# A linear attention block and an MLP on one core: another order of the same 1566 turns

## The chip, the core and the metric

The kernel runs on one core of a Trainium2 chip. The core has TensorE for matmuls (PE in the profile; its weight loads are PEld), VectorE (DVE), ScalarE (ACT), GpSimd (POOL), and SyncE (SP), whose queue here issues nearly all DMAs. Each engine works through its own list of instructions in order and waits on semaphores for the others. The metric is the device time of one execution in microseconds.

## The reference, cut to what matters

Gated linear attention keeps a 48x48 state per head, scaled by a gate and added to at every token; then a layer norm and a two-layer MLP with a residual. Four batches of 768 tokens, 8 heads of 48 (384 columns), 1536 hidden columns; the two weight matrices arrive as 64-bit floats.

```python
def _attn_ref(q, k, v, alpha):
    for t in range(S):
        state = alpha[:, :, t, :, None] * state + np.einsum('bhd,bhe->bhde', k[:, :, t], v[:, :, t])
        y[:, :, t] = np.einsum('bhd,bhde->bhe', q[:, :, t], state)

def _moe_ref(x, g_ln, w_ch1, w_ch2):
    mu = np.mean(x, axis=-1, keepdims=True)
    var = np.mean((x - mu) ** 2, axis=-1, keepdims=True)
    xn = (x - mu) / np.sqrt(var + 1e-06) * g_ln
    ch = np.maximum(xn @ w_ch1, 0.0) @ w_ch2
    return (x + ch).astype(np.float32)
```

## The kernel before

The tokens are cut into 6 chunks of 128 for each of 4 batches: 24 attention pieces, named a to x in time order (letter 4c + b for chunk c, batch b). A piece (`attention`, L278) takes the logarithm of its gates (ScalarE, L292), sums them along the tokens by a matmul with a triangle (L298 for chunk 0, L303 later), exponentiates (L306, L307), scales k and q (VectorE, L309, L311), transposes both (L336), forms scores (L352 or L360, one head a time), masks them (L367 or L372), updates the state (ups, L388; L397 or L401 and the gate's product on GpSimd, L403), forms the outputs (yps, L414, or L426 and L429), normalises (L437 to L470), transposes again (L476) and writes the columns of its chunk's xT (L479, L483). The gate of a chunk goes to DRAM as a row and comes back as columns (L316, L378).

The matmuls of single heads, L303, L352, L360, L388, L414, L426 and L429, use 64-row or 64-column tiles of the array, several of them side by side. All others use the whole array.

The MLP needs w1 and w2 in 32 bits. Twelve pieces (A to L: six of w1, then six of w2) are loaded by SP (L205) into three staging buffers and rounded by three VectorE operations, one on ScalarE (L223), and two more on VectorE (L217 to L227). Chunk 0 goes through the MLP in the plain way: hidden columns (L506, turns Y and Z) and projection (L518, turns P and Q). Chunks 1 to 5 use fast block products, with fewer products and more sums: 30 first products a chunk (L795, two matmuls each; turn M, and V for the last chunk) and 20 second products (L618, four matmuls each; turn M). The sums of inputs are VectorE operations on SBUF alone: `combine_first` (L744, S), `combine_x` (L769, X), `combine_weights` (L578, W), `combine_hidden` (L605, N). The sums behind a product read it from PSUM on VectorE or ScalarE (L628 to L678, L803 to L838), and some go on to GpSimd (L634, L814 to L834). R are the ReLUs (L846), O fetches the residual of an output (L493); finished outputs are sent at L497.

What sets the order is one string, ORDER (L25). Each of the functions named above is a generator, and a letter of the string runs its generator to its next `yield`:

```python
    with tc.manual_schedule():
        for turn in ORDER:
            next(turns[turn], None)
```

So the string fixes, for each engine, the order of its instructions, and for SP the order of its DMAs. Buffers rotate in the order in which turns ask for them. All PSUM tiles share eight buffers (`tag="bank", bufs=8`); la, x and xn share eight rows; qT, kT and the sums share eleven; alpha, k and q share six.

Of the kernel before, what the change touches and what calls it, by code (L numbers as in the profile page):

```python
# [22 lines left out]


ORDER = (  # L25
    "acacababcdaacabdbaabdcacabbacbbababceccbaAcfcdbadaacecacfeafdedebdfbeadbaedeecge"
    "adbAacgAfedghbgeedfecfafgfcefdAgeddbbgfdfghffbebaigcjbibffhjBhcdcYhCfcgccehYfedh"
    "cfedeedhgdedYjAfidBfjiBZhjhZZfBYegfhgjhghCiZYBYiCYYhfhghhkggZilihjZjgiZCiDjYDZZZ"
    "ghZYEYjkeiYkiDiEijgljjjlghYCYhiYkhYFEZhiFigYEZigkikDYZZlkkeejlYlgjhFlZlmYkZgknlg"
    "jZSGkHmiknlSljlkiljkjlGiHlmlllZimFhmZYgYmmjZiYhmheeHmGlkfSnZlnZefSQnmfiGHZghkkeo"  # L30
    "IYmSkiISkJgjIjommmOmJPJnSnQgopPghlKPIKhKjiPOnLSnSfSXkmQLffQOLXWkimXPQSWmPPXpnOpW"
    "XmnnXSmXSQomWnnpnmSoXmQMlmlkXkWliMnnMoXXpjWSWSMjMMoMoMlSMnMMWMoMknMMpMMqMMMMMOPi"
    "npnMopMMrmOMjkpMpopopRqoMoirQkplppnqprRppqWMMWMMnMWMqlMRrMMMMkMqRMMMjkrqRMrMMpsk"
    "oMoMMqMMRRnqpMMRjMqMMoWqOqsnRpqlsoqqpMsNtRNpMMNMjNoMoMMMosRqMMMOkNooMqtNMNMMMtMo"
    "MRlNNsmkNMpqMMNtMMMNlMrMMNMMNqMtqMsrMMWNnrrqMMMNMMstnMXvMsMMvXXprXorrXXXrqMMMXXM"
    "MMMMMMMsXqMMOmvMMMMMMMuXMMMMMMmtRMmttMRrtMrMMttrstvMtqussvsqtMMMMqMrMMrvMMMrRMMM"
    "MRMtMnMRMMmssmrMrrpOtsORMuRMoRMsMMMMoRNMMNtMMNMpqMMMoRNMRNMNNMMNRNOMnNMMMrstMpMN"
    "toNMNMMMMMrMnuoOMsMuNMvxMMuMNrpMOMNovMMvMMvMpMMMXtXMxvvMsXvssXXsXtvMXMuMXuXMMMMM"
    "usMMMtwMMMMMMvMMvwuuuRuuXuuuLxvXOMMMMMMMMMMMwMwxMrMuMswMuMMMwMMsvRxRvMMsMMRwMMxM"
    "xMqwMxMMxMwRtMMMxwMMMMxRqruwtxRwxswxxwRxwuxwRMNvNwMRMNrvwNRMMMMMMtNwNNquNNRrsvst"  # L40
    "tMNMJxMOMMMNNMxMMMvMqMuwxxMNtMtMMMMxuwXMwMMNXMXMMNMvNMXXuMXMXMMxXMXwMMXwMMMvMwMM"
    "MxMMMMMMMXMMMMMOuMuMMRMMMMMMMMwMMMMMMMMMRMMvxMMRMRxwMMMROMuMRMvOwxMMRRMwMRxMNMOM"
    "uMvMMXRVNMMMXXMMRMXXXXMMNVNVXVVXMVNMMVVVMVRVNXVVVVVNRVVMNXVVMVRVMVMVNVNMNVVVMVMV"
    "VMRVRVMVVVMVMVONVMVMNMVMMMRVMNNVRVVVVMVVROVMMMVMNVRVVRVMVMVMNMVRKMOMMMRNNMNMMNMM"
    "MMMNVNMNMNVMMMMNRONMMMNMMNMMMNMMMMNMMMNMMMMMMM"
)


# [860 lines left out]
```

## Time and profile before

| | |
|---|---|
| three runs | 434.07, 435.91, 436.53 us, median 435.91 |
| profiled execution, first to last instruction | 431.0 us; the page gives no other time for it, so its own time is known only by this span, 4.9 us under the median |
| TensorE busy | 425.7 us (99%) |
| weight loads busy | 378.2 us (88%) |
| VectorE busy | 333.2 us (77%) |
| ScalarE busy | 200.0 us (46%) |
| GpSimd busy | 152.7 us (35%) |
| granted TensorE clock | 0.999 |
| DMA | 45.53 MB; busy share 0.87 in the first 44 us, 0.64 from 44 to 120 us, 0.24 from 160 to 300 us |

The stages follow each other in TensorE's lines: the first hidden columns of chunk 0 (L506) start at 32.6 us, the projection of chunk 0 (L518) at 85.0, the first fast products (L795) at 123.6, the first second products (L618) at 161.9. Attention pieces lie among them until about 309 us.

A line of the profile names the engine, the line of the kernel and the tile; "x12" counts records, of which a matmul in 32 bits leaves two. The chain of work that ended last is followed back from the last instruction, at each step to what released it. A wait is idle time of an engine, put down to what ended it.

### The profile page before, as it was taken

The numbers are of one execution on the slowest core, as the hardware profiler recorded it, in microseconds if no ns is written. First come the engines' busy times: TensorE is split into PE (matmuls) and PEld (weight loads), VectorE is DVE, ScalarE is ACT, GpSimd is POOL, SyncE is SP. The second block draws the span as 40 slices with busy tenths as digits, with TensorE's granted clock in tenths as the row PEclk, the third lists the DMA queues.
The fourth block names the chain that finished last, engine by engine and source line by source line (L and its number), as shares of the span: only waits on it lengthen the run. The fifth ranks groups of instructions, "written<-read, shape, count | busy, mean of one in ns | idle before, by whom it ended". The sixth has DMA issues, their size and how long they took to land.

```text
span 431.0 us, 11676 instructions
## 1 busy us (share of the span) xinstructions
PE 425.7 (99%) x4760; PEld 378.2 (88%) x4760; DVE 333.2 (77%) x644; ACT 200.0 (46%) x519; POOL 152.7 (35%) x164
## 2 busy tenths in 40 slices
PE   8999999999999999999999999999999999999997
PEld 6788888866588889998889998889998899999996
DVE  4989899999998888866769756757686668948683
ACT  6597466774043882325385134384415562221100
POOL 1011031110205382252563243580153661647423
PEclk9999999999999999999999999999999999999999
DMA  8979968774117354031150141400014000011201
GB/s 287 288 208 272 308 151 257 203 247 142 38 56 212 107 148 141 29 105 45 52 151 23 49 120 38 94 2 22 2 56 146 2 1 2 0 39 37 75 18 55
DMA packets 55517, 45.53 MB, mean 106 GB/s; under 512 B 26748, under 2 KB 51580, under 8 KB 55464
## 3 DMA queue, kind: packets, MB, share of 16 engines
q1 hardware_dynamic: 54920, 44.63, 35.0%
q8 instruction: 37, 0.61, 0.6%
q10 hardware_dynamic: 544, 0.17, 0.2%
q14 instruction: 16, 0.13, 0.1%
HBM read 35.25 MB, written 9.53 MB: 104 GB/s over the span
## 4 chain that ended last, share of the span: by engine, by line
PE 94%; DVE 2%; DMA 1%; ACT 1%; SPq 0%; issue 0%; DVEq 0%
PE hps L795 30%; PE ops L618 30%; PE ops L518 7%; PE hps L506 6%; PE tps L336 4%; PE aps L360 3%; PE ups L388 2%; PE yps L426 2%; PE yps L429 2%; PE xps L476 2%; DMA ws<-in_moe_w_ch_dram 1%; PE lps L303 1%; PE aps L352 1%; PE lps L244 1%; PE lps L298 1%; PE yps L414 1%
## 5 line engine op out<-in xcount | busy, mean ns | idle before, releaser
L795 PE MATMUL hps<-sum,w 128*128 128x256 f32 x192 | 48.0, 381 | 0.0
L634 POOL TENSOR_TENSOR ob<-ob,u 128x192 f32<-128x192 f32 x40 | 27.0, 685 | 58.9 <-DVE ob L631 44.3
L618 PE MATMUL ops<-w,hT 128*128 128x192 f32 x224 | 40.7, 328 | 0.0
L795 PEld LDWEIGHTS hps<-sum,w 128*128 128x128 f32 x192 | 35.7, 190 | 4.7 <-ACT hT L825 0.2
L618 PEld LDWEIGHTS ops<-w,hT 128*128 128x128 f32 x224 | 36.9, 190 | 1.0 <-issue 0.6
L403 POOL TENSOR_TENSOR mid<-mid,gate 112x192 f32<-112x192 f32 x20 | 13.3, 668 | 68.7 <-DVE mid L401 19.7
L795 PE MATMUL hps<-xT,w 128*128 128x256 f32 x136 | 34.4, 380 | 0.0
L506 PE MATMUL hps<-xT,w 128*128 128x256 f32 x144 | 34.0, 384 | 0.1
L846 ACT ACTIVATE hT<-hT 128x512 f32<-128x512 f32 x48 | 28.8, 625 | 10.4 <-POOL hT L817 7.1
L518 PE MATMUL ops<-w,hT 128*128 128x384 f32 x96 | 32.8, 490 | 0.0
L628 DVE TENSOR_TENSOR ob<-ops,ob 128x192 f32<-128x192 f32 x50 | 17.6, 353 | 17.7 <-PE ops L618 9.4
L506 PEld LDWEIGHTS hps<-xT,w 128*128 128x128 f32 x144 | 26.3, 190 | 4.0 <-DVE xT L479 0.6
L618 PE MATMUL ops<-ws,sum 128*128 128x192 f32 x160 | 29.2, 327 | 0.0
L814 POOL TENSOR_TENSOR hT<-hT,u 128x512 f32<-128x512 f32 x8 | 10.4, 1305 | 53.0 <-DVE u L813 53.0
L795 PEld LDWEIGHTS hps<-xT,w 128*128 128x128 f32 x136 | 25.5, 190 | 3.2
L518 PEld LDWEIGHTS ops<-w,hT 128*128 128x128 f32 x96 | 17.6, 190 | 10.5
L618 PEld LDWEIGHTS ops<-ws,sum 128*128 128x128 f32 x160 | 26.4, 190 | 0.2
L336 PE MATMUL tps<-consts,qk 128*112 128x128 f32 x176 | 25.3, 275 | 0.2 <-DVE qk L311 0.2
L336 PEld LDWEIGHTS tps<-consts,qk 128*112 128x112 f32 x176 | 20.3, 134 | 4.3 <-DVE qk L311 0.8
L460 ACT ACTIVATE xn<-x,few 128x384 f32<-128x384 f32 x24 | 14.8, 615 | 18.7 <-DVE few L456 17.5
L618 PE MATMUL ops<-ws,hT 128*128 128x192 f32 x128 | 23.4, 327 | 0.0
L618 PE MATMUL ops<-more,sum 128*128 128x192 f32 x120 | 22.0, 327 | 0.0
(243 smaller groups left out, 1172.9 us busy)
## 6 DMA issues: line engine op xcount, KB each, us to landing
ws<-in_moe_w_ch_dram SPq DMA_DIRECT2D x12, 768.0 KB
vn<-in_v_dram SPq DMA_DIRECT2D x12, 384.0 KB
kept<-x SPq DMA_DIRECT2D x24, 192.0 KB
ob<-kept SPq DMA_DIRECT2D x24, 192.0 KB
out_dram<-ob SPq DMA_DIRECT2D x19, 192.0 KB
ra<-in_alpha_dram SPq DMA_DIRECT2D x14, 192.0 KB
rk<-in_k_dram SPq DMA_DIRECT2D x6, 384.0 KB
rq<-in_q_dram SPq DMA_DIRECT2D x6, 384.0 KB
```

The lines of the kernel that those rows point to most:

```text
L336: nc.tensor.transpose(tps[:, p], qk_of(c, b)[:, i, p].rearrange("p a b -> p (a b)")[:, :R], ident)
L360: nc.tensor.matmul(aps[0][halves[i if cross else 1 - i], p, s], kT[rs, p, s], qT[rs, p, s], start=True, stop=True)
L403: nc.gpsimd.tensor_mul(new, new, by)
L460: act(out=xn, in_=x, func=AFT.Square, bias=mean, accum_out=dev)
L506: nc.tensor.matmul(hps, w1[:, j // 2, f, j % 2 * P:][:, :P], xT_of[0][:, f, bs], start=(f == 0), stop=(f == NF - 1))
L518: nc.tensor.matmul(ops_of[b], hT_of[c][:, j, b], w2[:, j], start=(j == 0), stop=(j == NJ - 1))
L618: nc.tensor.matmul(acc, lhs[:, j], rhs[:, j], start=(j == 0), stop=(j == NT - 1))
L628: nc.vector.tensor_add(x, acc, x)
L634: getattr(nc.gpsimd, f"tensor_{op}")(x, x, y)
L795: nc.tensor.matmul(acc[:, i], w, b, start=True, stop=True)
L814: add_late(c4, c4, u2)
L846: nc.scalar.activation(out=x, in_=x, func=AFT.Relu)
```

## The change

Only the string is another one. Both strings hold the same letters equally often. The letter changes at 1258 of the 1565 places between two turns in the old string and at 854 in the new one, where a letter often stands many times in a row. The new order was chosen with VectorE and GpSimd allowed to work side by side. Cut to a few rows, the first, two of the middle and the last:

```diff
-    "acacababcdaacabdbaabdcacabbacbbababceccbaAcfcdbadaacecacfeafdedebdfbeadbaedeecge"
-    "adbAacgAfedghbgeedfecfafgfcefdAgeddbbgfdfghffbebaigcjbibffhjBhcdcYhCfcgccehYfedh"
...
-    "MRlNNsmkNMpqMMNtMMMNlMrMMNMMNqMtqMsrMMWNnrrqMMMNMMstnMXvMsMMvXXprXorrXXXrqMMMXXM"
-    "MMMMMMMsXqMMOmvMMMMMMMuXMMMMMMmtRMmttMRrtMrMMttrstvMtqussvsqtMMMMqMrMMrvMMMrRMMM"
...
-    "MMMNVNMNMNVMMMMNRONMMMNMMNMMMNMMMMNMMMNMMMMMMM"
+    "acaabaaaabbdbbbcdccaaacabbbadbeaccfbbbabcccceafecdadefAfaabdaabacaaeeaddfdedbeae"
+    "eacccgdddbeAehfgggcebgcbbbhddgdecfAefffgbggbAefefefgdfggffffggBdCjhjccAhcdcYdhdg"
...
+    "MMMMWMNNjjMMrrlqnNNsMMMMMrpnMtNoqMrtqqmrrrnrorrjrtrtrMMMMlooOMNtssjsjmNMXXXXXXXX"
+    "XpMrmMMMMMMMMMsMMvMMMMMrqppMppuMMMXOMMMMMMMtttsstsLsssssvttttXtRtrrttsuuvvRuutsM"
...
+    "OMMMMMMMMMMMMMMMMMOMMMMMMMMMMMMMNNNMMMMMMMMMMM"
```

Since each engine's list follows the string, every engine's list changes its order: TensorE's 2512 matmuls, VectorE's 634 instructions, ScalarE's 471, GpSimd's 164 and SP's 259 DMAs. The products of one chunk keep their order among themselves (`FIRST`, L775, and `SECOND`, L609), as do the operations of one attention piece and of one piece of weights.

## The prediction

> **What bounds the kernel now.** I read the page first: busy times, the 40 slices, the chain that ended last.
>
> ```profile
> PE 425.7 (99%) x4760; PEld 378.2 (88%) x4760; DVE 333.2 (77%) x644; ACT 200.0 (46%) x519; POOL 152.7 (35%) x164
> ...
> PE   8999999999999999999999999999999999999997
> ...
> DVE  4989899999998888866769756757686668948683
> ...
> POOL 1011031110205382252563243580153661647423
> ...
> PE 94%; DVE 2%; DMA 1%; ACT 1%; SPq 0%; issue 0%; DVEq 0%
> ```
>
> TensorE is busy 425.7 of 431.0 us and holds 94% of the chain. A busy PE need not be working at full rate, so I then read what it waited for (the waits with TensorE as the one that waits; this is the whole answer):
>
> ```profile
> PE lps L244 <- DVE more L241: 1.1, 1, 1.1
> PE aps L352 <- DVE kT L341: 0.8, 1, 0.8
> PE tps L336 <- DVE qk L311: 0.2, 1, 0.2
> ```
>
> 2.1 us in all, all before 12 us. Third, the pieces of the chain in order of time. From 43.85 us to 427.9 us every piece is a PE piece. What they show is a price that no wait table has:
>
> ```profile
> 52.60 5.18 PE hps L506 x24
> 59.80 2.79 PE hps L506 x12
> 62.59 1.10 PE yps L426 x58
> ...
> 80.46 2.59 PE hps L506 x12
> ...
> 169.09 0.66 PE lps L303 x3
> ...
> 256.68 0.93 PE yps L426 x58
> ...
> 307.04 1.08 PE yps L429 x64
> 308.12 1.04 PE yps L426 x61
> 309.16 1.50 PE ops L618 x8
> 310.98 11.70 PE ops L618 x72
> ```
>
> Twelve hps records take 2.59 us when what stands before them uses the whole array (the transposes of L336 and L476), but 2.79 behind a run of the small matmuls of one head (59.80). Eight ops records take 11.70 / 72 x 8 = 1.30 in the stream and 1.50 behind small ones (309.16). So coming back from small tiles costs 0.20 us. Going in costs between nothing (1.08 for 64 records first in a run, 1.04 for 61 second) and 0.17 (1.10 for 58 first in a run, 0.93 for 58 inside one). The end is fixed: last VectorE add at 428.0 + 0.36, then 2.6 us until the last output lands.
>
> **The change, part by part.** No instruction is added or removed: 2512 matmuls, 507 VectorE two-tensor operations, 156 GpSimd ones, 259 DMAs from SP in both.
>
> *Fewer changes of tile size.* In the instruction order, the small matmuls (L303, L352, L360, L388, L414, L426, L429) stand in 29 unbroken runs before and 16 after; mean length by the chain's rates goes from some 2.1 to 3.7 us. 13 returns at 0.20 and 13 entries at 0 to 0.17: 2.6 to 4.8 us. I take 0.28 a pair, the middle, since both entry rows occur: 13 x 0.28 = 3.6 us, all of it on the path, since PE is the path. One more run ends with L303 (4 against 3), whose last pair then lies bare (169.09: 0.66 us) where inside a run it overlaps its neighbours: 0 to 0.6 us back, taken as 0.3.
>
> *Longer runs need more banks at once.* All PSUM tiles share eight buffers (tag "bank"). A run with two chunks' lps, aps, two ups and two yps fills them, and the first big product behind it waits for an eviction. Evictions by rows: copy_predicated (L372) 0.73 us, the yps sum (L443) 0.55, the state adds (L401) 0.35. Walking the new order with these durations, there are some eight places, from about 70 us on, where the eviction that frees the bank (or the yps before a projection) stands right ahead of the matmul that needs it. The price of each is between nothing and one whole late eviction, 0.73: 0 to 5.8 us. I take 0.2, nearer the low end, because the order before also has such pairs and no wait on PE came of them: 8 x 0.2 = 1.6 us. What hides it where it costs nothing is VectorE's spare time, 101 of 140 us busy between 160 and 300 us; between 44 and 120 us (70.8 of 76.0) there is hardly any.
>
> *VectorE and GpSimd side by side.* The trace of before shows that they are not free of each other. Two-tensor VectorE operations on SBUF alone, and GpSimd's:
>
> ```profile
> L605 DVE TENSOR_TENSOR sum<-sum,sum x15: 681/684/1539, 174.2 to 423.4; 128x512 f32<-128x512 f32 x15
> ...
> L605 DVE TENSOR_TENSOR sum<-sum,hT x4: 682/884/1757, 185.0 to 389.1; 128x512 f32<-128x512 f32 x4
> ...
> L634 POOL TENSOR_TENSOR ob<-ob,u x40: 587/591/1242, 179.9 to 426.9; 128x192 f32<-128x192 f32 x40
> ```
>
> The columns are minimum, median and maximum in ns. 1757 is 684 plus most of a 1270 ns GpSimd add (L814's median is 1276); VectorE operations that read PSUM keep their time beside GpSimd. A collision so costs the late engine up to 1.3 us, and the order before already has them without a wait on PE. Laying the operations of both orders side by side at their places among the matmuls, 57 two-input operations fall beside a GpSimd one before and 48 after, so I see no more collisions, only less distance where one falls. Bounds: -0.5 (a few fewer) to 8.7 us (worked out below); taken 0, since the count gives no more of them. The Trainium skill, page "SBUF — State Buffer", section "Who interferes with whom", says that a VectorE instruction with two SBUF inputs and a GpSimd instruction that reads SBUF hold one shared read interface in turn, the second fully blocked: it speaks against a plan that lets them run side by side. The 684 and 1757 ns agree with it. By that rule alone each collision costs its whole overlap; by the waits above it costs PE nothing until it meets a short distance.
>
> *The head.* First transposes wait for the same q load (VectorE's 8.03 us operation): 8.7 us against 8.64. The kT copies now stand ahead of the third k product, so the first L352 can start 0.6 us earlier than 11.47. The weight loads keep their places in SP's queue: pieces 0 to 5 are SP's 22nd, 47th, 53rd, 55th, 67th and 68th DMA (before: 20, 47, 55, 62, 65, 73). Piece 3 goes ahead of the alpha, k and q of a chunk, so those are up to 2.6 us late (768 KB at the 308 GB/s of the page's busiest slice); between load and first use the new order leaves them 6 us or more of PE work at that place. Piece 1's rounding has six VectorE operations between its halves instead of three, some 1.4 us more, against a PE use that is 3 us of matmuls behind. Ends: -0.6 to +2.6 us, taken 0, being hidden on the rows just named. SP's queue loses no DMA, and what waits behind a blocked one there is what waited before. The tail has the same last products and the same sends: 0.
>
> *Sum.* -3.6 + 0.3 + 1.6 = -1.7 us on the profiled span: 431.0 to 429.3. The median of the three runs is 435.9, 4.9 above the span; I leave that alone: 435.9 - 1.7 = 434.2 us.
>
> **The rivals.**
>
> *All of the saving arrives.* If no bank is late, only 13 pairs count: -3.6, with the entries dear -4.8, minus 0.3 for L303: 432.3, down to 431.4. For it: VectorE has a quarter of its time free after 160 us. Against: between 44 and 120 us it has 7% free.
>
> *Slower, by blocked operations.* One mechanism: a GpSimd add of 1.27 us starts just ahead of a VectorE operation on SBUF that the next matmul needs, once in each half of each of the five later chunks (first products L795, second products L618). With 0.4 us of distance at such a place, 10 x (1.27 - 0.4) = 8.7 us, less the saving: 435.9 - 3.6 + 0.3 + 8.7 = 441.3; at half the places 437.0. It decides from about six places on (438.1). For it: the plan that chose the order is the one that lets the two run side by side, and 1757 ns rows exist. Against: the count of 57 and 48. The shared-interface rule of "SBUF — State Buffer" is what would make this one come true.
>
> *Slower, by loads.* The chunk's alpha behind piece 3 lands 2.6 us late where ScalarE needs it, and the weight pieces behind it likewise: two such waits and no head start give 435.9 - 3.3 + 1.6 + 5.2 = 439.4. For it: DMA engines are 87% busy in the first 44 us. Against: the order leaves each weight load at least 4.1 us of PE work to its first rounding, before 2.7.
>
> *Longer runs choke on banks.* At 0.73 for half of the eight places and 0.2 for the rest the saving is gone: 435.9 - 3.3 + 3.7 = 436.3, no change. The Trainium skill, "TensorEngine Tiling (Array Packing)", section "Gotcha 1: PSUM Pressure", warns that row tiles raise the pressure on PSUM banks. No wait in this trace shows it, with runs of 2.1 us.
>
> **How the numbers follow.** Chances: 0.42 for the forecast (434.2, its own range 433.0 to 435.4), 0.20 for the whole saving (432.3), 0.12 for no change (436.3), 0.16 for blocked operations, 0.10 for loads. The bound of 0.5% is 2.2 us (433.7 and 438.1), about what a measurement of this kernel can tell from no change: the three runs shown differ by 2.5. Below 433.7 lie the whole saving and 0.17 of the forecast's 0.42: faster 0.37. Same: the other 0.25 and the 0.12: 0.37. Slower: 0.16 + 0.10 = 0.26. The range 431.8 to 439.0 leaves out about 0.04 below and 0.14 above.
>
> **What would show it.** In the chain of the changed kernel, about 16 pieces of hps or ops should carry the extra 0.20. The waits of PE should hold new rows of some tenths, for evictions (L372, L401, L443, L483) right behind long small runs; if there are none, the saving arrives whole. VectorE's maxima on L605 and L769 and GpSimd's on L634 say whether collisions grew: their busy sums are 333.2 and 152.7 now, and 10 us more on either would be the sign. The first L795 should start by about 123 us (now 123.6). It is wrong if PE shows single waits of over a microsecond after 44 us, or if small matmuls don't run at the same rate in long runs.

## The result, and the profile after

| | before | after |
|---|---|---|
| median of four runs each, beside each other | 434.99 us | 448.43 us |
| ratio, with its 95% interval | | 1.0304 (1.026 to 1.0347): slower by 3% |
| profiled execution, first to last instruction | 431.0 us | 446.2 us |
| first L506 / L518 / L795 / L618 | 32.6 / 85.0 / 123.6 / 161.9 us | 34.0 / 90.7 / 134.5 / 171.2 us |
| last product ends | 427.9 us | 443.1 us |

The forecast was 434.2 us with a range of 431.8 to 439.0. The new order is 13 us slower, far outside it. (The medians and ratios leave out executions with a mean granted clock of 0.66 to 0.95, one that took twice the time, and two that lay over 1.5% above the fastest of their kernel: 446.0 us in experiment 11 and 457.4 in experiment 13.)

I read the page of the new order as before: the busy times, the 40 slices, the chain that ended last.

```profile
PE 432.7 (97%) x4760; PEld 383.7 (86%) x4760; DVE 335.2 (75%) x644; ACT 204.1 (46%) x519; POOL 149.1 (33%) x164
...
PE   7998999999989999999999999998999999999997
...
DVE  3998788889958879948676966676766669857964
...
PEclk9999899999999999999999999999999999999999
...
PE 87%; DVE 6%; issue 2%; POOL 2%; DMA 1%; SPq 0%; ACT 0%; DVEq 0%; POOLq 0%
```

TensorE is still the busiest by far, but it lost 7 points of the chain: to VectorE, to GpSimd and to "issue", time in which the engine waited for nothing that the profile names. The slice marked 8 in PEclk (the fifth) had no counterpart before. VectorE's and GpSimd's busy sums hardly moved (333.2 to 335.2, 152.7 to 149.1). TensorE's waits, the whole answer; the order before had three rows and 2.1 us, all ahead of 12 us:

```profile
PE ups L388 <- issue: 2.4, 2, 1.9
PE lps L298 <- ACT la L292: 1.5, 1, 1.5
PE yps L429 <- issue: 1.5, 1, 1.5
PE lps L244 <- DVE more L241: 1.1, 1, 1.1
PE yps L426 <- DVE x L443: 0.9, 1, 0.9
PE ops L618 <- DVE ob L628: 0.8, 1, 0.8
PE hps L795 <- ACT hT L825: 0.7, 1, 0.7
PE ops L618 <- DVE sum L605: 0.7, 2, 0.4
PE tps L336 <- DVE qk L311: 0.6, 1, 0.6
PE hps L506 <- issue: 0.2, 1, 0.2
```

The columns are the total in us, how often, and the longest. The largest rows have no releaser. In the chain in order of time (start, length, what), two of them look like this:

```profile
42.11 0.09 PE ups L388 x4
42.20 1.93 issue
44.13 0.49 PE ups L388 x15
44.62 2.31 PE hps L506 x6
...
127.59 1.25 PE yps L429 x83
128.84 1.46 issue
130.30 0.84 PE yps L429 x42
...
131.20 0.66 PE lps L303 x6
```

Three things are to be seen. The stop stands in the middle of a run of one kind of matmul, and the profile names nothing that it waits for. Behind the first, six hps records take 2.31 us, where they take 1.30 in the stream. And at the end of the second run six lps records (L303) take 0.66 us, the price that the prediction had read at 169.09 us of the order before.

Summed by line, as the time from each matmul's start to the next one's, the small matmuls (L303 to L429) went from 62.0 to 74.1 us, the big ones from 364.5 to 367.6. So most of the loss lies inside the runs of small matmuls, which the prediction had taken as unchanged. It is not a slower rate: leaving out steps of over 0.12 us, small matmuls of one line follow each other as before (17 ns at L388, 16 at L426, 15 at L429; at L360 27 instead of 25). The steps of over 0.12 us within the runs sum to 3.2 us before and 14.3 after: stops, and triangle sums.

From these traces I made three theories. **A, bare triangle sums:** the two halves of an L303 pair lie on two quadrants of the array; next to score turns (L360) that use the other two quadrants they run at the same time as these, elsewhere they stand bare. The groups that stood bare were 3 of 18 before (at 17, 32, 169 us) and 10 of 18 after; the time at L303, from the start of each record to the next matmul's, sums to 3.60 and 8.19 us. **B, instruction supply:** TensorE uses its instructions faster than they arrive. The queue that carries them (q8, 37 packets of 16,384 bytes, one for every 256 of TensorE's instructions) had a transfer just ahead of each stop: one started at 41.62 us, took 1.39, and the stop ended 1.12 us after it. **C, late operands and blocked operations:** the rest of the table, the rival of the prediction.

### The profile page after: what moved, and what is told of

Read it like the earlier page. It is cut to its first block, busy times and chain, and to the rows that moved or that the text cites. A ratio compares the mean times of both kernels' runs of the same rounds, so it can differ in the third digit from the quotient of the medians.

```text
span 446.2 us, 11664 instructions
## 1 busy us (share of the span) xinstructions
PE 432.7 (97%) x4760; PEld 383.7 (86%) x4760; DVE 335.2 (75%) x644; ACT 204.1 (46%) x519; POOL 149.1 (33%) x164
## 4 chain that ended last, share of the span: by engine, by line
PE 87%; DVE 6%; issue 2%; POOL 2%; DMA 1%; SPq 0%; ACT 0%; DVEq 0%; POOLq 0%
PE hps L795 26%; PE ops L618 24%; PE hps L506 7%; PE ops L518 7%; PE tps L336 5%; PE aps L360 4%; PE ups L388 3%; PE yps L429 2%; PE yps L426 2%; PE lps L303 2%; DVE sum L605 2%; PE xps L476 2%; DMA rq<-in_q_dram 1%; PE aps L352 1%; PE yps L414 1%
## 5 line engine op out<-in xcount | busy, mean ns | idle before, releaser
L634 POOL TENSOR_TENSOR ob<-ob,u 128x192 f32<-128x192 f32 x40 | 26.0, 660 | 83.3 <-DVE ob L631 64.1
L795 PE MATMUL hps<-sum,w 128*128 128x256 f32 x192 | 47.9, 380 | 0.0
L795 PEld LDWEIGHTS hps<-sum,w 128*128 128x128 f32 x192 | 35.9, 190 | 5.5 <-DVE mid L401 0.6
L618 PE MATMUL ops<-w,hT 128*128 128x192 f32 x224 | 40.0, 327 | 0.4 <-DVE sum L605 0.4
L618 PEld LDWEIGHTS ops<-w,hT 128*128 128x128 f32 x224 | 36.8, 190 | 1.2 <-DVE sum L605 0.6
L403 POOL TENSOR_TENSOR mid<-mid,gate 112x192 f32<-112x192 f32 x20 | 11.5, 580 | 70.1 <-DVE mid L401 51.8
L795 PE MATMUL hps<-xT,w 128*128 128x256 f32 x136 | 34.6, 381 | 0.0
L506 PE MATMUL hps<-xT,w 128*128 128x256 f32 x144 | 34.0, 390 | 0.2 <-issue 0.2
L846 ACT ACTIVATE hT<-hT 128x512 f32<-128x512 f32 x48 | 27.7, 623 | 13.2 <-POOL hT L833 5.5
L518 PE MATMUL ops<-w,hT 128*128 128x384 f32 x96 | 32.3, 488 | 0.0
L506 PEld LDWEIGHTS hps<-xT,w 128*128 128x128 f32 x144 | 27.0, 192 | 5.2 <-DVE at L372 0.6
L618 PE MATMUL ops<-ws,sum 128*128 128x192 f32 x160 | 28.7, 327 | 0.3 <-DVE sum L605 0.3
L795 PEld LDWEIGHTS hps<-xT,w 128*128 128x128 f32 x136 | 25.5, 190 | 3.3
L518 PEld LDWEIGHTS ops<-w,hT 128*128 128x128 f32 x96 | 17.7, 190 | 11.6 <-issue 0.6
L618 PEld LDWEIGHTS ops<-ws,sum 128*128 128x128 f32 x160 | 26.3, 190 | 0.6 <-DVE sum L605 0.6
L336 PE MATMUL tps<-consts,qk 128*112 128x128 f32 x176 | 24.2, 281 | 0.6 <-DVE qk L311 0.6
L360 PE MATMUL aps<-qT,kT 48*64 48x64 f32 x640 | 24.4, 221 | 0.0
L360 PEld LDWEIGHTS aps<-qT,kT 48*64 48x64 f32 x640 | 21.8, 134 | 2.4 <-issue 1.4
L618 PE MATMUL ops<-ws,hT 128*128 128x192 f32 x128 | 23.5, 327 | 0.0
```

The lines of the kernel that those rows point to most:

```text
L336: nc.tensor.transpose(tps[:, p], qk_of(c, b)[:, i, p].rearrange("p a b -> p (a b)")[:, :R], ident)
L360: nc.tensor.matmul(aps[0][halves[i if cross else 1 - i], p, s], kT[rs, p, s], qT[rs, p, s], start=True, stop=True)
L403: nc.gpsimd.tensor_mul(new, new, by)
L506: nc.tensor.matmul(hps, w1[:, j // 2, f, j % 2 * P:][:, :P], xT_of[0][:, f, bs], start=(f == 0), stop=(f == NF - 1))
L518: nc.tensor.matmul(ops_of[b], hT_of[c][:, j, b], w2[:, j], start=(j == 0), stop=(j == NJ - 1))
L618: nc.tensor.matmul(acc, lhs[:, j], rhs[:, j], start=(j == 0), stop=(j == NT - 1))
```

## The experiments

Compared are medians; the kernel before, run beside each, lay between 434.4 and 435.2 us.

### 1. The triangle sums among the scores

Eleven turns of the string move, with what directly hangs on them; three of them:

```diff
 r's second turn (L303):  "...kWMo[r]ooooo..."  ->  "...oooop[r]ppoo..."
 s's second turn:         "...qqqq[s]sMpM..."   ->  "...RMqq[s]qqqq..."
 u's second turn:         "...rtts[u]uvvR..."   ->  "...ttss[u]tsLs..."
```

> The new order, but eleven of the pairs of L303 (the triangle sums of pieces h, j, m, n, p, q, r, s, t, u, w) stand between two score turns (L360) whose tiles use the two other quadrants of the array. Nothing else moves but the exps that follow directly. Theory A (a pair that stands bare costs TensorE 0.65 to 0.86 us, a pair between such scores lets its neighbours run at the same time): in the new order ten groups stand bare, eight of them are mended here; the eight matmuls from the first L303 on take 0.9 to 1.0 us bare and 0.53 inside, so 8 x 0.45 = 3.6 us less: 444.8 us against 448.4 for the new order. The sum of the spans of L303 falls from 7.85 to about 3 us. Rival (the place of L303 is of no account, the time is lost to late operands or to instruction supply): 448 us, or more, since sums that are held longer take a bank.

Measured: 444.80 us (443.87 to 447.33), ratio 1.0230 (1.018 to 1.028). The chain at the same place, first the new order, then this kernel:

```profile
148.32 0.65 PE lps L303 x4
148.97 0.52 PE aps L360 x18
```

```profile
148.22 0.06 PE lps L303
148.28 0.29 PE aps L360 x11
148.57 0.05 PE lps L303
```

The lps records no longer hold up the scores. The sum of L303's time from start to start fell by 4.8 us, from 8.19 to 3.42, but that of L360 rose by 2.7, from 17.7 to 20.4: a net 2.1 us in these two traces. By the medians the kernel is 3.6 us faster, by runs of equal granted clock (below) 2.3 us. Theory A holds, as a part of the 13 us.

The move has a price that I overlooked. The stop at 42 us now has a releaser:

```profile
PE ups L388 <- ACT x L437: 2.0, 1, 2.0
```

ScalarE takes an output out of its bank (L437) at 44.0 us, where the new order did so at 41.1. Four exps stand ahead of it, and they wait for the moved triangle sum until 42.4 us. So this is no stop of the supply (it lies 16 instructions ahead of the boundary) but a wait for a bank: with eight banks in rotation, the second of the two ups tiles takes the one that this output held. The prediction had called this longer runs needing more banks at once. The expectation of experiment 5 takes it for a stop at a boundary.

### 2. Three runs cut

```diff
 hAPS1 ... hAPS2      + first turn Z between them (it stood behind the run)
 nUPS  ... kYPS       + one turn Q (it stood ahead of the run)
 kYPS  ... mYPS       + one turn P (it stood behind the run)
 sUPS  ... tAPS0, tAPS3 ... rYPS   + two turns M each (ahead of the run)
```

The names are those of the turns: hAPS1 is the second score turn of piece h, UPS its state update, YPS its outputs.

> The new order with big products moved into the three runs of small matmuls that stopped with no wait named (at 42.2, 128.8 and 220.4 us): one turn Z into the first, one turn Q and one turn P into the second, two products M into the third. Theory B (in a long run TensorE uses its instructions faster than they are fetched, and after the 1.9 us stop the granted clock falls): the three stops, 1.93 + 1.46 + 0.47 us, go, and with them the slow products at 44 to 48 us, 1.0 to 1.7 us; four more returns and entries at 0.28 cost 1.1: 448.4 - 3.9 - 1.3 + 1.1 = 444.3 us. Rival (the stops are late operands that the trace does not name): the stops stay in the same length, at the same instructions, and the time is 448.4 + 1.1 = 449.5 us.

Measured: 446.67 us (446.63 to 450.01), ratio 1.0289 (1.023 to 1.0348), between the two expectations; at a granted clock of 1.000 it is 446.6 against 446.2 for the new order (below), so nothing was won. The stops at 128 and 220 us were gone, the one at 42 us was 1.2 instead of 1.9. But at the first L795 a new wait stood, 2.0 us for a sum of VectorE (L769). The chain there:

```profile
130.89 0.71 PE lps L303 x7
...
131.62 0.49 ACT eq L306
132.11 0.39 ACT lps L307
...
132.52 0.56 DVE qk L309
133.08 0.47 DVE qk L311
133.54 0.60 DVE w L744
...
134.52 0.44 DVE sum L769
...
135.09 1.10 PE hps L795 x4
```

VectorE's queue stands at L309, which waits for the exps of a triangle sum that the string put at the very end of the run; the sums of the next product stand behind it. The time won at the stops was lost there. So B's stops could be removed, but not the time: in the new order a second limit lies close under the first, VectorE's order behind long runs.

### 3. Outputs twelve times over

```diff
-        for p in range(NP):
+        for p in [p for _ in range(12 if (c, b) in ((2, 0), (4, 0)) else 1) for p in range(NP)]:
```

> The kernel before, with the output matmuls (L429 and their partners, 64 records) of the pieces (chunk 2, batch 0) and (chunk 4, batch 0) issued twelve times over, each time into the same place: two runs of 768 records of small matmuls, with nothing to wait for. One repetition takes 0.95 to 1.05 us in the kernel before, so at full rate the two runs take 23 us and the kernel 435 + 21 = 456 us. Theory B (instruction supply): each fetch brings 16,384 bytes, 256 instructions, which two repetitions use up in 1.9 to 2.1 us; in the three stops of the new order TensorE went on 2.3 to 2.65 us after the start of a fetch. So after the first two to four repetitions there is a stop of 0.4 us or more at every second repetition, named as issue, each ended some 1 to 1.4 us after a fetch has landed: 8 to 10 stops, 4 to 15 us more, 460 to 471 us. Rival (no such limit; the stops in the new order have another cause): twelve even repetitions, no stop, 456 us.

Measured: 476.87 us in one run, and TensorE's wait at the outputs, named as issue, is 14.7 us in 10 stops. The second run in the chain:

```profile
217.96 1.61 issue
219.57 2.08 PE yps L429 x128
221.65 1.38 issue
223.02 2.08 PE yps L429 x128
225.10 1.65 issue
226.75 2.08 PE yps L429 x128
```

Exactly 128 records, with their weight loads 256 instructions, and then a stop, with nothing to wait for. The stops of this run of outputs end 3.45 and 3.73 us apart, in turn, though TensorE needs 2.08 us for a block; the instruction queue carried 48 packets instead of 37. Theory B is shown. The stops lie at the upper end of what was expected (14.7 us, 4 to 15). The time lies above the expected 460 to 471 us, and the clock accounts for it: it was 0.50 from 82 to 92 us, behind the first stops, and fell again behind the run shown (the last three numbers are the granted clock, the DMA share and GB/s):

```profile
234.00:238.00 4.00, 4.00 (x120) 3.91 (x121) 0.00 (x0) 0.00 (x0) 0.00 (x0) 0.70 0.01 4
```

The mean of 0.985 over 474.8 us stands for some 7 us: 456 + 14.7 + 7 = 477.7 us, where 476.87 were measured.

With this I numbered TensorE's instructions in program order (a matmul in 32 bits is two loads and two matmuls, a transpose one of each, and the waits that stand alone in its list one). All ten stops here lie at numbers that leave 194 over from 256. So do, within one, those of the new order: 1473, 3778, 6081, 7875 and 8130 leave 193, 194, 193, 195, 194. The last two I had put down to late sums, since the profile names VectorE there (`yps L426 <- DVE x L443` and one of `ops L618 <- DVE sum L605`); they lie at boundaries in the other traces of this order too, and each time a fetch had landed 1.2 to 1.6 us ahead of the end, so a part of them at least is supply.

### 4. The old order, then the new

The old order's first 503 letters, then the letters that are left in the sequence of the new string.

```diff
-    "XmnnXSmXSQomWnnpnmSoXmQMlmlkXkWliMnnMoXXpjWSWSMjMMoMoMlSMnMMWMoMknMMpMMqMMMMMOPi"
+    "XmnnXSmXSQomWnnpnmSoXmQiiijSlnnnnnolkllqkqkkppkMSqSkkmMooXnXkMMMMMMMMMMMMMlMMMMM"
+    "MProomMpmXpOORpMpQkMMkWMoroooooopppooppnppqpoMlMOqWqMRMMnrMMpRRMmMppWmMMMMMWWMMM"
...
```

> The old order up to its first M turn, then the new order for all turns that are left. By the traces the new order is 10.9 us later at the first L795 and 4.3 us more behind it. If the two parts lose their time on their own (bare sums, instruction supply and late operands at their places), this order loses only the second part: 435.0 + 4.3 = 439.3 us, 438 to 441. If the second part loses what it loses because the first came late, or the other way round, it is below 437 or above 443.

Measured: 442.94 us (439.89 to 443.83), ratio 1.0166 (1.0114 to 1.0217), above the expected 438 to 441. From the first L618 to the last product it took 271.0 us; the new order 271.9, the order before 266.0. So the second part loses 5 to 6 us also behind the old first part. The total is 3.6 us above the expected, probably because the first L795 is no clean border (a part of the small matmuls left over from the new string's first part stands behind the seam), and because the profiled execution was already 3.4 us late at the first L518, in an order that is the same up to there.

### 5. Triangle sums and cuts together

```diff
 as 1, and
 hAPS1 ... + first turn Z;  hAPS3 ... + second and third turn Z
 nUPS ... + one turn Q;  sUPS ..., tAPS3 ... and vYPS ..., wUPS ...  + two turns M each
```

> The new order with both changes: the eleven pairs of L303 among the scores as in the first experiment, and products moved into the runs where that experiment still stopped at a boundary of 256 instructions (two turns Z at 42 us, one turn Q at 128, two products M each at 218 and at 304 us). Its stops there were 2.2 + 0.45, 1.6, 0.9, 0.6 and 0.4 us, 6.1 in all; seven more entries and returns at 0.28 cost 2.0. Theory B (instruction supply): 444.8 - 6.1 + 2.0 = 440.7 us, and no stop of over 0.5 us behind 40 us. Rival (VectorE's order is the bound underneath: what stands behind a late operation of an attention piece in its queue comes late, so the time won at a stop is lost at the next product): 443 to 445 us, with waits of TensorE for VectorE's sums in the place of the stops, as the 2.0 us for L769 in the second experiment.

Measured: 445.8, 447.6 and 448.1 us; ratio 1.0294 (1.0245 to 1.0343). A miss: it is slower than experiment 1 by some 3 us, and above even the rival's range. The only trace, at a clock of 0.85, has no stop without a releaser over 0.5 us behind 40 us, but TensorE waiting 2.1 us for ScalarE's ReLU (L509) and 1.1 for xn (L470). At L509 the chain goes back over ScalarE's four exps to the moved triangle sum, as at 42 us in experiment 1. So the 2.2 us that the expectation counts there were never a stop of the supply, and cutting the run could not win them. The rest of the miss stays open.

### 6. The old order behind 176 more instructions

```diff
-    for _ in range(8):
-        nc.tensor.matmul(idle[:, :P], zero, zero, start=True, stop=True)
+    for h, n in [(slice(0, P), P)] * 4 + [(slice(0, 64), 32), (slice(64, P), 32)] * 24:
+        nc.tensor.matmul(idle[h, :n], zero[h, :h.stop - h.start], zero[h, :n], start=True, stop=True)
```

> The order of the kernel before, unchanged, with 176 more TensorE instructions ahead of it: of the eight idle matmuls of the warm-up (L244) four stay, and 48 very small ones are added, which end at about the same time as before. All stops so far lay at instruction numbers of TensorE's program that leave 193 to 195 over from 256. Theory B: the boundaries now fall on other places of the same order. With 3.75 us from the entry into one block of 256 to the first instruction of the next, and an entry 28 instructions ahead of execution (both fitted to the stops of the new order), the stops come out as 1.7 us at 126.7 us (L388), 0.95 at 143.8 (L795), 1.5 at 257.3 (L426) and 1.5 at 291.4 us (L426), in times of the profile of before: 435.2 + 5.6 = 440.8 us. Rival (the kernel before has no stops because its runs are shorter, wherever the boundaries lie): 435.2 us, no stop.

Measured: 439.78 us, ratio 1.0123 (1.009 to 1.0155). The number is as expected, the reason is not. The small matmuls took 58 ns a record, so the first L298 came at 8.32 us instead of 4.62 and the first L506 at 37.9 instead of 32.6: by these two traces that is the whole difference. Of the four stops two came, at 149.2 us (0.4 from start to start) and 297.3 us (0.8), both at the forecast instructions and both at 193 over from 256, but smaller; two did not. Between the first L506 and the last product lay 396.7 us against 395.3. Refitted to all stops so far, as an estimate, an instruction is entered about 50 ahead of its execution and the next block is there 3.75 us after the entry into the one ahead of it.

### 7 and 8. Without GpSimd's sums, in both orders

```diff
-            getattr(nc.gpsimd, f"tensor_{op}")(x, x, y)
+            pass
...
-        add_late, sub_late = nc.gpsimd.tensor_add, nc.gpsimd.tensor_sub
+        add_late = sub_late = lambda o, x, y: nc.gpsimd.tensor_add(o, x, y) if o is not x else None
```

> The new order without the sums that GpSimd adds in place: all of L634, and of L814 to L834 all but the first of the two at L820, 100 of GpSimd's 110 sums; the output lacks them. The gate's products on GpSimd (L403) stay. Theory of blocked operations (VectorE's sums wait for GpSimd's): the new order loses most of its 13.4 us that way, so it falls here to 437 to 441 us, and the order before, without the same sums, stays within 1 us of its 435. Theories A and B: what is lost is lost on TensorE's side; the new order falls by 0 to 2 us only (446.4 to 448.4), the order before by as much.

> The control of the run without GpSimd's sums: the order before without the same 100 sums. 433.5 to 435.2 us by theories A and B, 434.2 to 436 by the theory of blocked operations; what tells the two apart is the difference between the two kernels: 13.4 us as with the sums, or 2 to 6 us.

Measured: the new order 442.50 us (441.73 to 444.81), ratio 1.0196 (1.015 to 1.0241); the order before 434.25, ratio 1.0007 (0.9982 to 1.0033). The order before gains nothing, the new one 5.9 us. That is between the two expectations, and more than theories A and B allowed: the rival of blocked operations has a real part. The stops in the second half that lie at no boundary are gone with it (at 181.8, 206.2 and 425.1 us: 0.3, 0.7 and 0.8 us); 271.9 us from first L618 to the end became 268.2. The last of them in the chain of the new order:

```profile
410.80 1.61 POOL at L821
...
412.43 0.04 DVE at L827
...
414.84 1.10 DVE qk L605
415.95 1.70 DVE sum L605
...
425.51 0.36 DVE ob L628
...
425.92 0.43 PE ops L618
```

VectorE waits for GpSimd's L821, then runs 13 us without a pause until a sum that TensorE waits for. Its waits at L827 for L821 were 4 before (6.2 us) and 9 after (10.8 us).

```profile
L821 POOL TENSOR_TENSOR at<-at,at x2: 1602/1677/1752, 393.8 to 410.8; 128x512 f32<-128x512 f32 x2
```

This row (minimum, median, maximum in ns) had 1268/1302/1337 before. So in this stretch the two engines did hold each other up: GpSimd's sum was slower by 0.4 us, and the piece of L605 at 415.95 is one record of 1.76 us, beside GpSimd's L834 (415.4 to 417.1), where such a sum alone takes 0.68. Which part of the 5.9 us is such blocking and which is plain waiting for GpSimd's result in a worse sequence, this experiment can't tell, since it takes both away. Nor is all of it GpSimd's: in this trace the stops at 42 and 128 us are 1.3 and 1.1 us instead of 1.9 and 1.5, and the clock stayed at 1.000; at equal clock (below) the gain is 3.8 us.

### 9. The new order once more

> The new order unchanged, on the same chip as the three runs beside it, as the value that they are compared with. 448.4 us if chips agree; its second part, from the first L618 to the last product, 271.9 us in the first trace (266.0 in the order before).

Measured: 446.1, 449.1 and 450.8 us, ratio 1.0317 (1.0249 to 1.0386). With the first four runs these make seven, and they sort by the mean granted clock that each run carries: 446.1 and 446.3 us at 1.000; 448.0 and 449.1 at 0.996; 448.9, 450.1 and 450.8 at 0.992. The order before ran at 0.999 or 1.000 in all its undisturbed runs. So five of seven runs of the new order had a lower clock, and were 2 to 5 us longer. Where, shows in the first trace (a stretch, its length, busy time of PE, PEld, DVE, ACT and POOL, and then the granted clock, the DMA share and GB/s):

```profile
42.00:44.00 2.00, 0.20 (x12) 0.08 (x5) 1.75 (x4) 1.05 (x2) 0.00 (x0) 1.00 0.96 327
44.00:46.00 2.00, 1.87 (x25) 1.59 (x25) 1.34 (x3) 0.00 (x0) 0.00 (x0) 0.79 1.04 392
46.00:48.00 2.00, 2.00 (x10) 1.70 (x8) 1.97 (x3) 0.18 (x1) 0.00 (x0) 0.50 1.04 343
48.00:50.00 2.00, 2.00 (x14) 1.95 (x14) 1.93 (x6) 1.27 (x4) 0.00 (x0) 0.86 0.96 307
```

After the stop of 1.93 us the clock falls to half for about 3 us: 0.21 + 0.50 + 0.14 of three 2 us stretches, 1.7 us lost. That is 0.004 of the span, the step between the three groups.

### 10. Triangle sums, and cuts without the turns Z

```diff
 as 5, without
 hAPS1 ... + first turn Z;  hAPS3 ... + second and third turn Z
```

> The eleven pairs of L303 among the scores, and cuts as in the fifth experiment but without the two turns Z at 42 us (there TensorE waited 2.1 us for ScalarE's ReLU L509 and 1.1 for xn instead): one turn Q at 128, two products M each at 218 and at 304 us. Of the stops of the first experiment 1.6, 0.9, 0.6 and 0.4 us go, five entries and returns at 0.28 come: 444.8 - 3.5 + 1.4 = 442.7 us by theory B. If what VectorE and ScalarE do late is the bound underneath, 444 to 446.

Measured: 446.64 us (446.38 to 452.21), ratio 1.0301 (1.0229 to 1.0373). A miss as well. In the trace (of the slowest of the four runs) the stops at 128, 218 and 304 us are gone as meant; but a stop of 2.6 us, from start to start, stands at a boundary at 32 us, where experiment 1, with the same letters up to there, had 1.5. The granted clock behind it was 0.50 from 34.7 to 41.5 us, 3.4 us lost, which is most of what this run lies above the other three. The 2.0 us for ScalarE's L437 are there as in experiment 1, and there are waits for ScalarE (xn 1.2, kT 0.7) that experiment 1 did not have. Cutting the runs of this order brought nothing, and why the other three runs are slower than experiment 1 stays open.

### 11. Triangle sums, and without GpSimd's sums

```diff
 as 1 and 7
```

> The eleven pairs of L303 among the scores, and without the 100 sums on GpSimd (the output lacks them). Alone the first gave 444.8 us, the second 442.5, against 448.4. If they are two separate losses, 448.4 - 3.6 - 5.9 = 438.9 us, 438 to 440, and what is left above the order before without these sums (434.3) is the instruction supply: stops of 1.3 to 1.6 us at 42 and 127 us and 0.5 us each at 217, 301 and 305 us. If one covers for the other: 441 to 443 us.

Measured: 439.1, 442.4 and 443.0 us, ratio 1.0141 (1.0061 to 1.0221). The runs at a granted clock of 1.000 give 446.2 for the new order, 443.9 with the triangle sums moved, 442.4 without GpSimd's sums (middle of three), 439.1 with both: 2.3, 3.8 and 7.1 us, which would make them separate losses. But 439.1 is a single run; the median of 442.4 us misses the expected 438 to 440 and lies where one loss covers for the other. In the trace of that run the 2.0 us for ScalarE's L437 stand at 41 us, and the clock was 0.50 from 43.3 to 46.7 us. So it stays open how far the two add up.

### 12. The old order, shifted once more

```diff
-    for _ in range(8):
-        nc.tensor.matmul(idle[:, :P], zero, zero, start=True, stop=True)
+    for o, n in [(slice(0, P), P)] * 2 + [(halves[0], 32), (halves[1], 32)] * 23:
+        nc.tensor.matmul(idle[o, :n], zero[:, :o.stop - o.start], zero[:, :n], start=True, stop=True)
```

> The order of the kernel before once more behind a shifted warm-up, since in the sixth experiment the 48 small matmuls took 3.7 us longer than what they replaced and so moved all that followed. Now two of the eight wide idle matmuls stay and 46 small ones on the whole height of the array are added: 160 more TensorE instructions. Refitted to all stops so far (3.75 us from entry to the next block, entry 50 instructions ahead of execution) theory B gives three stops, in times of the profile of before: 1.5 us at 126.8 (L388), 1.4 at 259 (L426) and 1.35 at 294 us (L426); in the sixth experiment such stops came at 0.4 to 0.8 of what this fit gives. So 2 to 4.2 us more between the first L506 and the last product, which are 395.3 us apart in the kernel before: 397.3 to 399.5 us, and 436.4 to 438.6 us in all if the warm-up ends as early as before. Rival: no stop, 395.3 and 434.4 us.

Measured: 440.8, 441.1 and 442.0 us, ratio 1.0148 (1.0099 to 1.0197). Inconclusive: the warm-up ended at 7.2 us instead of 4.6, and the only trace is one at a clock of 0.66, so the share of the stops can't be read. It shows two of the three forecast stops, at L388 (0.3 us) and L426 (0.5 us), 193 and 194 over from 256.

### 13 and 14. Both orders behind 48 more instructions

```diff
+    for o, n in [(slice(0, P), P)] * 4 + [(halves[0], 32), (halves[1], 32)] * 8:
```

> The new order, unchanged, behind a warm-up of the same length with 48 more TensorE instructions: four of the eight wide idle matmuls (L244) stay, 16 small ones are added; by the 58 ns that a small record took in the sixth experiment they end within 0.3 us of the old ones. Only the places of the boundaries of 256 instructions move. Theory B, with 3.75 us to the next block and entry 50 instructions ahead, gives stops of 0.5 us at 41.6, 0.9 at 68.6, 0.6 at 84, 1.2 at 130, 0.9 at 306 and 1.7 us at 309 in times of the profile of the new order: 5.9 us in all against 2.8 by the same fit with the boundaries where they were, so 3.1 us more: 448.6 + 3.1 = 451.7 us. If the places of the boundaries are of no account: 448.6 us.

> The same warm-up ahead of the order before. Theory B gives stops of 0.6 us at 64.7, 1.2 at 77.5 and 1.3 at 294 us, where it gives none with the boundaries in their old places, and none are in the trace: 434.6 + 3.1 = 437.7 us, or 436 to 437 if the stops are at 0.4 to 0.8 of the fit as in the sixth experiment. If the places of the boundaries are of no account: 434.6 us, no stop.

Measured: the order before 436.89 us (436.43 to 440.25, seven runs), ratio 1.0078 (1.0048 to 1.0108): 2.4 us slower, with an unchanged order and a warm-up that ends 0.3 us later. Two of the three forecast stops are there, at the forecast places, and the instructions leave 193 over from 256:

```profile
78.21 0.44 PE ups L388 x21
78.66 1.05 issue
79.71 0.30 PE ups L388 x3
...
295.30 1.01 issue
296.31 0.47 PE ups L388 x10
```

The new order: 448.4, 451.5, 452.6 and 454.4 us, ratio 1.0397 (1.0352 to 1.0443). Their middle, 452.1, lies 3.2 us above the middle of the seven runs of the unshifted new order, 448.9, where 3.1 were expected (its two ratios were 1.0304 and 1.0317); at a granted clock of 1.000 it is 448.4 against 446.2. Two runs of the shifted old order had a granted clock of 0.996 (439.2 and 440.3 us), which no undisturbed run of the unshifted one has. So the place of the boundaries against the runs of small matmuls costs time by itself: shown for the old order, by the times and the trace. For the new order the times fit, but the intervals of the ratios touch, and no trace of an ordinary run shows its stops. That the stops bring the lower clock with them is likely from the counts of runs, not shown.

## Why the prediction was wrong

*Fewer changes of tile size.* The mechanism and its size were right. 16 runs came as counted. A pair costs 0.32 us where I took 0.28: going in 0.09, the last small matmul 0.13 longer, coming back 0.10, the same at nearly every place of both traces. 13 x 0.32 = 4.2 us were saved.

*The step that failed* stands in the same part: "mean length by the chain's rates goes from some 2.1 to 3.7 us". It takes for granted that small matmuls run at the same rate in a long run. The prediction named this as what would make it wrong, and it did. Between the stops the rate was the same, but runs of up to 7.9 us hold up to 704 instructions, and a block of 256 takes TensorE 2.1 us while the next arrives 3.5 to 3.75 us after the entry into the last. In the profiled execution the stops at boundaries come to 5.4 us (1.9 + 1.5 + 0.5 named as issue, and 0.2, 0.9 and 0.4 at three boundaries more, of which a part may be late sums), and the lower clock behind the first to 1.7. That such stops cost time is shown by experiments 3 and 14; that the new order would be faster by as much without them is not, since cutting the runs won nothing. The trace of before held no such stop, and the line of the instruction queue on its page, 37 packets, was not read. The old order has long runs too, but they lie well against its boundaries: 48 instructions further, and it has two stops.

*Bare L303.* "One more run ends with L303", 0.3 us, counted only the ends of runs, from the rule that "inside a run it overlaps its neighbours". The runs showed that it overlaps only next to score turns on the other two quadrants: seven more bare groups, 4.6 us at L303 in the trace, 2.3 to 3.6 when eight were mended.

*Longer runs need more banks.* One wait of the list is of this kind: yps behind VectorE's L443, 0.9 us, at a place where a boundary lies too. The other places showed none; in this order 1.6 us was too much rather than too little. Experiment 1 shows that the mechanism is real: there ScalarE's late L437 stopped TensorE for 2.0 us.

*VectorE and GpSimd side by side, taken 0.* Wrong: the new order gains 3.8 to 5.9 us without GpSimd's sums, the old one nothing; of that blocking is a part, whose size stays open. That the busy sums did not grow fits the count of 57 and 48 pairs, but it answered the wrong question: a collision counts by what waits behind it, as in the chain from L821 to the product at 425.92 us. The rival priced this mechanism at 441.3 us, with a chance of 0.16.

*The head.* First transposes came at 9.7 us instead of 8.6; but three other traces of the old order had them at 9.7 to 9.9 too, so this is scatter between executions. The term of 0 stands. The profiled execution of before was a quick one: where a run has both, its time is 1.7 to 2.2 us above its span, so its time was some 433 us, and some 3 of the 4.9 us that the prediction left alone were scatter too.

*The sum.* In the traces: 4.2 us saved, and lost 4.6 (bare L303, an upper bound by experiment 1), 5.4 (stops), 1.7 (clock), 1.8 (late operands of the second half), 1.0 (head): 10.3 of the 15.2 us between the spans. Some 5 us stay unassigned. Experiment 2 showed late operations of VectorE right under a stop, and 5 and 10 gained nothing by cutting; how much of the loss would be left with every stop gone stays open. The baseline of 435.9 us was 0.9 high against the four runs, which changes nothing. One slip: with its own 0.3 for L303 the whole saving gives 432.6 us, not 432.3.

## What to carry to other kernels

A busy engine that waits for nothing can still be short of instructions: count the instructions of a stretch against its length before making it denser, and where small matmuls come in hundreds, look how their runs lie against the blocks of 256. Spreading big matmuls among them took stops away here, but won no time while other late operations stood close behind. What overlaps in one order need not in another: before taking a row's price along with a move, look which neighbours made it cheap. And in a queue that is worked through in order, the place of an operation that waits counts more than how often two engines meet.

## What the runs showed of the hardware

TensorE's instructions arrive in blocks of 256. In the third experiment one block came 3.45 to 3.73 us after the other at the least; of the small matmuls of this kernel 256 instructions take 2.08. The Trainium skill, page "Runtime: NRT & Kernel Launch", section "Instruction fetch mechanics", says that the sequencer fetches the next block of 256 instructions while it executes the one at hand, and that this is mostly hidden. The trace agrees with the blocks (16,384 bytes a packet, stops 256 instructions apart); that it is hidden holds in the order before, and not in the third experiment, where at the second run of outputs one block after the other left a stop of 1.4 to 1.7 us.

Between 42 and 50 us of the new order, where the DMA share is 0.96 to 1.04, a block came later: block starts at 39.1 and 44.1 us lie 5.0 us apart. In experiment 1 the fetch at 30.0 us took 2.06 us where most take 0.9 to 1.5. That the data transfers are the cause is not shown.

Behind stops of 2 us the granted clock can halve for 3 us or more: 0.50 from 46 to 48 us in the new order, 0.50 from 82 to 92 us in the third experiment, and 0.70 on the mean from 234 to 238 us, right behind its second row of stops, after 1.00 from 218 to 234. It need not: behind the 2.0 us of experiment 1 it stayed at 1.00. The Trainium skill, page "TensorE: Matmul & The Clock Gate", section "Part 1: The HAM clock gate (the "warmup" mystery)", names half speed as the idle state, entered after an idle window of about 3.4 us. The half agrees; in this trace TensorE had been idle for 1.93 us only.
